# First casts off GpSimd, weights prepared later, scores of a head pair in two halves: fused attention and gated unit on one core

## Chip, cores and metric

One core of a Trainium2 chip. The metric is device time in microseconds (us) of one execution of the program, the median of several runs; one more execution was recorded by the profiler.

## What is computed

Attention over 8 batches, 8 heads, 576 positions and 64 channels, causal by blocks of 64 positions, and behind it a gated unit on the attention output laid out as 512 channels:

```python
scores = scale * np.matmul(q, k.transpose(0, 1, 3, 2))
scores = np.where(mask, scores, -1000000000.0)      # mask: block_i >= block_j
...
x = attn_out.transpose(0, 2, 1, 3).reshape(B, S, H * D)
for k in range(5):
    gate_pre += conv_w[k] * xp[:, k:k + S, :]       # xp: x with 4 rows of zeros ahead
out = (sigmoid(gate_pre) * (x @ w_val)) @ w_out
```

## The kernel before

The work is cut into 32 **steps**; step t handles one pair of heads of batch t // 4. Query and key arrive in **blocks** of four heads (`load_pair`, L393): a block feeds two steps, so steps 0 and 1 need block 0, steps 2 and 3 block 1, and so on. A load (`load_qk`, L90) is two DMAs on SyncE's queue and a cast from fp32 to fp16 (L99), on GpSimd but for the first. `load_v` (L102) is one DMA and eight copies of GpSimd, once per batch. `trans` (L121) turns a third of a block with TensorE (L129), and VectorE copies the result out of PSUM (L135).

A step's `scores` (L149) fill four PSUM buffers one after the other, of which two exist at a time; ScalarE takes the exponential of each (L163 twice at 1024 columns, L186 at 512, L163 at 320). When four steps are done, `den` (L206) sums the exponentials of the batch with 88 small matmuls (L237), and VectorE turns the sums into reciprocals, split in two bf16 parts (L244 to L249, ending in `comb`). `recips` (L253) spreads them with two matmuls per step (L259) that ScalarE copies out (L261), and `pv` (L265) makes the attention output, five steps behind the scores. `gate_val` (L314), nine steps behind, does the convolution as matmuls with diagonal weights (`diag`, L324), the gate (L327) and the value projection (L332); `project` (L340) the last product. All PSUM tiles but those of the scores come from one pool of four buffers (`psG`).

Before the loop stand the first two blocks, the first transposes, `consts`, `load_v(0)` and `weights` (L371): two weight loads on ScalarE's queue, a cast of each on GpSimd (L389), the convolution weights turned by four small fp32 matmuls (L375) and the 20 diagonal matrices (L380, GpSimd). In the loop (L427) come in turn the load of the next block, `load_v` of the next batch, the scores, the transposes of the block that follows, and `after` (L406).

The functions say what is done; a scheduler puts each engine's instructions into a fixed order, by its own estimates, when the program is built. At run time each engine works through its list in order, so an instruction that must wait holds up all behind it.

## Time and profile before

| | us |
|---|---|
| median of 3 runs | 287.13 |
| lowest, highest | 285.99, 287.56 |
| profiled execution, whole | 287.68 |
| profiled execution, span of the trace | 285.9 |
| TensorE busy in the span | 243.7 (85%) |
| ScalarE busy | 157.4 (55%) |
| VectorE busy | 143.6 (50%) |
| GpSimd busy | 102.7 (36%) |

PE is TensorE's matmul, PEld its weight load, DVE is VectorE, ACT ScalarE, POOL GpSimd, SP SyncE; a name with q behind it is the engine's queue. Times inside the trace count from the start of the span. A row of the timeline gives start, busy time, engine, line, operation, tiles, shape and count, and in brackets how long the engine had been idle and what ended that.

### The profile page before, as it was taken

The page shows a single profiled execution, that of the slowest core. Times are in us where ns is not written, and L with a number is a line of the kernel's source. Part 1 is how long each engine was busy: PE and PEld are TensorE (multiplying, and loading weights), DVE is VectorE, ACT ScalarE, POOL GpSimd, SP SyncE. Part 2 cuts the span into 40 slices and gives each one's busy share as a digit, 9 for nine tenths or more (in the row PEclk, how much of TensorE's full clock was granted, in tenths as well). Part 3 has the DMA queues.
Part 4 walks back from the last instruction along what each step waited for, and adds up shares of the span by engine and source line. Part 5 has one row for each costly group of instructions (what it writes and reads, how often), then busy time and mean ns, then how long its engine had stood idle before and what let it go on. Part 6 is the DMA issues. An engine that isn't in the chain of part 4 may idle for free.

```text
span 285.9 us, 7361 instructions
## 1 busy us (share of the span) xinstructions
PE 243.7 (85%) x3128; PEld 160.4 (56%) x3128; DVE 143.6 (50%) x257; ACT 157.4 (55%) x293; POOL 102.7 (36%) x129
## 2 busy tenths in 40 slices
PE   1672198796999998999899998999899999999994
PEld 1530164563666556666557556755667557667671
DVE  3730074579356835594438644683539324634230
ACT  1064048585476375728574575637584875444433
POOL 7379999917521911264113811182000000000000
PEclk9999999798699999999999999999999999999998
DMA  6999687999638587226933240001200210121214
GB/s 200 332 261 367 129 257 214 274 269 271 184 113 214 156 206 236 85 85 174 291 120 101 78 156 2 2 33 42 76 37 2 77 73 5 73 76 38 77 72 183
DMA packets 24842, 40.32 MB, mean 141 GB/s; under 512 B 1765, under 2 KB 10981, under 8 KB 24810
## 3 DMA queue, kind: packets, MB, share of 16 engines
q1 hardware_dynamic: 18560, 28.32, 35.2%
q10 hardware_dynamic: 6250, 11.55, 11.1%
q8 instruction: 24, 0.39, 0.6%
q14 instruction: 8, 0.07, 0.1%
HBM read 30.42 MB, written 9.44 MB: 139 GB/s over the span
## 4 chain that ended last, share of the span: by engine, by line
PE 58%; DVE 12%; ACT 11%; DMA 6%; issue 5%; POOL 3%; SPq 2%; ACTq 1%
PE cv L324 14%; PE vp L332 10%; PE ot L343 7%; PE x L304 7%; ACT pt L163 7%; PE ps L159 6%; DMA st<-in_k_dram 6%; PE dn L237 5%; DVE qkT L135 4%; PE tr L129 4%; ACT ob L347 3%; DVE hi L245 2%; SPq L95 2%; DVE ri L244 2%; POOL diag L380 1%
## 5 line engine op out<-in xcount | busy, mean ns | idle before, releaser
L163 ACT ACTIVATE pt<-ps 128x1024 f16<-128x1024 f32 (+1 forms) x96 | 77.7, 834 | 26.7 <-PE ps L159 23.8
L135 DVE COPY qkT<-tr 128x768 f16<-128x768 f16 (+1 forms) x64 | 50.3, 836 | 44.6 <-PE tr L129 44.4
L99 POOL CAST t<-st 128x1152 f16<-128x1152 f32 x31 | 35.1, 1145 | 69.3 <-PE tr L129 63.3
L336 DVE SCALAR_TENSOR_TENSOR gv<-th,vp 128x288 f16<-128x288 f32 x64 | 28.9, 452 | 35.0 <-PE vp L332 34.0
L129 PE MATMUL tr<-ident_59,t 128*128 128x128 f16 x288 | 26.6, 244 | 21.5 <-POOL t L99 15.1
L159 PE MATMUL ps<-qkT 64*128 64x64 f16 (+7 forms) x256 | 37.2, 312 | 7.6 <-ACT pt L163 4.5
L327 ACT ACTIVATE th<-cv 128x288 f32<-128x288 f32 x64 | 26.1, 415 | 31.5 <-PE cv L324 31.2
L347 ACT COPY ob<-ot 128x512 f32<-128x512 f32 x36 | 21.1, 585 | 36.5 <-PE ot L343 34.5
L324 PEld LDWEIGHTS <-diag 128*128 128x128 f16 x320 | 29.0, 98 | 15.9 <-issue 7.3
L343 PE MATMUL ot<-w_out_sb,gv 128*128 128x512 f16 x144 | 34.7, 380 | 1.7 <-DVE gv L336 1.7
L129 PEld LDWEIGHTS <-t 128*128 128x128 f16 x288 | 19.3, 109 | 27.9 <-POOL t L99 16.3
L304 PE MATMUL x<-pt,t 128*64 128x256 f16 (+3 forms) x384 | 30.7, 260 | 3.7 <-DVE qkT L135 3.0
L261 ACT COPY rb<-ps 128x288 f32<-128x288 f32 x64 | 23.6, 409 | 11.3 <-PE ps L259 10.9
L332 PEld LDWEIGHTS <-w_val_sb 128*128 128x128 f16 x256 | 25.0, 98 | 6.8
L186 ACT ACTIVATE pt<-ps 128x512 f16<-128x512 f32 x32 | 19.4, 605 | 14.3 <-PE ps L184 12.7
L304 PEld LDWEIGHTS <-t 128*64 128x64 f16 x384 | 18.8, 112 | 11.8 <-issue 6.6
L108 POOL CAST t<-st 128x2304 f16<-128x2304 f32 x8 | 16.9, 2106 | 20.5 <-PE x L304 18.3
L343 PEld LDWEIGHTS <-gv 128*128 128x128 f16 x144 | 13.7, 98 | 16.6 <-DVE gv L336 3.7
L159 PEld LDWEIGHTS <-qkT 64*128 64x128 f16 x256 | 11.7, 97 | 19.6 <-issue 13.4
L244 DVE RECIPROCAL ri<-dn 128x288 f32<-128x288 f32 x8 | 15.7, 1958 | 8.8 <-PE dn L237 8.5
L306 DVE TENSOR_TENSOR xb_69<-x,rb 128x320 f16<-128x320 f32 (+1 forms) x24 | 10.1, 444 | 17.0 <-ACT rb L261 15.3
L324 PE MATMUL cv<-xb_69,diag 128*128 128x288 f16 x120 | 18.4, 300 | 0.0
(93 smaller groups left out, 332.1 us busy)
## 6 DMA issues: line engine op xcount, KB each, us to landing
st<-in_q_dram SPq DMA_DIRECT2D x32, 288.0 KB, 3.9
st<-in_k_dram SPq DMA_DIRECT2D x32, 288.0 KB, 4.4
out_dram<-ob ACTq DMA_DIRECT2D x36, 256.0 KB, 2.0
st<-in_moe_w_val_dram ACTq DMA_DIRECT2D x1, 1024.0 KB, 9.9
st<-in_moe_w_out_dram ACTq DMA_DIRECT2D x1, 1024.0 KB, 7.4
st<-in_v_dram SPq DMA_DIRECT2D x8, 0.2 KB, 9.3
conv_nat<-in_moe_conv_w_dram ACTq DMA_DIRECT2D x1, 10.0 KB
```

Source lines behind the costliest of these rows:

```text
L99: eng.tensor_copy(out=t[:, :, :, :], in_=st[:, :, :, :].rearrange("p z c d -> p c z d"))
L129: nc.tensor.transpose(out=tr[:, s, :], in_=q16[hb, w][:, c, :, :], identity=ident16[:, :])
L135: nc.vector.tensor_copy(out=qkT[b][:, 2 * half:2 * half + 2, w, :].rearrange("p n (x c) -> p n x c", c=9)[:, :, :, c0:c0 + len(ss)], in_=t ...
L159: mm(out=ps[:, h, lo:lo + S - f], lhsT=kT[h][:, f - 64:f + 64], rhs=qT[h][:, f:S], start=True, stop=True, skip_group_check=True)
L163: nc.scalar.activation(out=pt[:, o:o + w], in_=src, func=AF.Exp, bias=0.0, scale=0.125)
L304: mm(start=(z == 0), stop=(z == len(x_) - 1), skip_group_check=True, **x_[z])
L324: mm(out=cv[:, :], lhsT=diag[:, g, j, :], rhs=xb[:, g, HF * hf + j:HF * hf + j + HF], start=(j == 0), stop=(j == 4), skip_group_check=True)
L327: nc.scalar.activation(out=th[:, HF * hf:HF * hf + HF], in_=cv[:, :], func=AF.Tanh, bias=0.0, scale=0.5)
L332: mm(out=vp[:, :], lhsT=w_val_sb[:, fc, 128 * g:128 * g + 128], rhs=xb[:, fc, 4 + HF * hf:4 + HF * hf + HF], start=(fc == 0), stop=(fc == ...
L336: nc.vector.scalar_tensor_tensor(out=gvs[u][:, g, c0:c0 + HF], in0=th[:, HF * hf:HF * hf + HF], scalar=1.0, in1=vp[:, :], op0=ALU.add, op1 ...
L343: mm(out=ot[:, :], lhsT=gvs[u][:, fc, 128 * j:128 * j + 128], rhs=w_out_sb[:, fc, :], start=(fc == 0), stop=(fc == 3), skip_group_check=True)
L347: nc.scalar.copy(out=ob[:, :], in_=ot[:, :])
```

## The change

The key cast of block 0 goes to ScalarE (the query cast was on VectorE already). `weights` is split: the convolution weights are prepared at step 3, with the 20 diagonal matrices on VectorE in place of GpSimd; the two large weights are loaded on SyncE's queue, the first at step 2 and the second at step 4. The second block's load and `load_v(0)` are asked for behind the first transposes. `scores` is called twice per step: two PSUM buffers first, then, behind the transposes, `recips`, `den` and `pv`, the other two.

```diff
-        eng = nc.vector if hb == 0 and w == 0 else nc.gpsimd
-        eng.tensor_copy(out=t[:, :, :, :], in_=st[:, :, :, :].rearrange("p z c d -> p c z d"))
+        cast = (nc.vector.tensor_copy, nc.scalar.copy)[w] if hb == 0 else nc.gpsimd.tensor_copy
+        cast(out=t[:, :, :, :], in_=st[:, :, :, :].rearrange("p z c d -> p c z d"))
...
-    def scores(t):
+    def scores(t, part):
...
+        if part == 0:
+            ps = psS.tile([128, 2, 512], fp32, tag="S")
+            full(ps, 0, 0, 0)
...
+            ex(1024, ps[:, :, :], 1024)
+            return
...
-                nc.gpsimd.tensor_scalar(out=diag[:, g, j, :], in0=ident16[:, :],
+                nc.vector.tensor_scalar(out=diag[:, g, j, :], in0=ident16[:, :],
...
+    def weights(w):
...
+        nc.sync.dma_start(out=st.rearrange("p (f n) -> p f n", f=4),
...
+    nc.scalar.dma_start(out=conv_nat[0:5, 0:512], in_=moe_conv_w[:, :])
     load_pair(0)
-    load_pair(1)
     for part in range(3):
         trans(0, part)
+    load_pair(1)
+    load_v(0)
     consts()
-    load_v(0)
-    weights()
...
+    for t in range(NT + 9):
         b, r = divmod(t, 4)
+        if t < NT:
+            scores(t, 0)
+        if t % 2 == 0:
+            load_pair(t // 2 + 2)
+        if t in (2, 4):
+            weights(t // 2 - 1)
+        if t == 3:
+            conv_weights()
+        if r == 1 and b + 1 < B:
+            load_v(b + 1)
+        if t < NT and t // 2 + 1 < 2 * B:
+            for part in ((0, 1), (2,))[t % 2]:
+                trans(t // 2 + 1, part)
+        if 0 <= t - 5 < NT:
+            recips(t - 5)
         if r == 0 and 1 <= b <= B:
             den(b - 1)
         if 0 <= t - 5 < NT:
-            recips(t - 5)
             pv(t - 5)
+        if t < NT:
+            scores(t, 1)
```

Three places show what this does to the fixed orders. The first is GpSimd's list before, from the casts of block 0's keys and block 1 (L99) to those of blocks 2 and 3.

```order
L99 CAST t<-st 128x1152 x3
L389 TENSOR_SCALAR w_val_sb<-st 128x2048
L380 TENSOR_SCALAR diag<-ident_59,convT 128x128 x3
L108 CAST t<-st 128x2304
L110 CAST d<-st 64x1024
L112 CAST d<-st 64x4x64 x4
L114 CAST vz_72<-st 64x4x320
L115 CAST vz_72<-st 64x4x64
L380 TENSOR_SCALAR diag<-ident_59,convT 128x128 x17
L389 TENSOR_SCALAR w_out_sb<-st 128x2048
L99 CAST t<-st 128x1152 x4
```

The same list now, from the last of the eight copies of batch 0's values on; ahead of it stand the two casts of block 1 and the other seven copies.

```order
L115 CAST vz_72<-st 64x4x64
L99 CAST t<-st 128x1152 x2
L108 CAST t<-st 128x2304
L110 CAST d<-st 64x1024
L112 CAST d<-st 64x4x64 x4
L114 CAST vz_73<-st 64x4x320
L115 CAST vz_73<-st 64x4x64
L99 CAST t<-st 128x1152 x2
L391 TENSOR_SCALAR w_val_sb<-st 128x2048
L99 CAST t<-st 128x1152 x2
L391 TENSOR_SCALAR w_out_sb<-st 128x2048
```

Block 2's casts moved ahead of all weights, but block 3's now stand behind the copies of batch 1's values, which they were ahead of.

The second place is TensorE's list where `den` of batch 0 begins; before, with the transposes of block 3 (tr_473) ahead of it and step 3's third score buffer (ps_403) amid it:

```order
L129 LDWEIGHTS t_343
L129 MATMUL tr_473<-ident16_59,t_343 128x128
L237 LDWEIGHTS oh_60
L237 MATMUL dn_482<-pt_242,oh_60 32x5x32
...
L237 MATMUL dn_482<-pt_242,oh_60 32x256
L159 LDWEIGHTS qkT_146
L159 MATMUL ps_403<-qkT_146 128x256
```

Now the same place follows the last score buffer of step 5 (ps_655) and the first transposes of block 3 (tr_449):

```order
L197 MATMUL ps_655<-qkT_328 64x64
L129 LDWEIGHTS t_318
L129 MATMUL tr_449<-ident16_59,t_318 128x128
...
L240 LDWEIGHTS oh_60
L240 MATMUL dn_466<-pt_200,oh_60 32x5x32
```

Steps 4 and 5 moved from amid and behind `den` of batch 0 to ahead of it. In the same way step 9's scores, which stood behind `den` of batch 1, stand ahead of it now, all but its last two small matmuls.

The third place is VectorE's list around the diagonal matrices (L382), between the copies of blocks 1 and 2 (ahead) and of block 3 (behind), as it is now:

```order
L135 COPY qkT<-tr 128x2x64x6 x2
L135 COPY qkT<-tr 128x2x64x3 x2
L379 COPY convT<-ps 128x20
L135 COPY qkT<-tr 128x2x64x6
L382 TENSOR_SCALAR diag<-ident_59,convT 128x128 x20
L135 COPY qkT<-tr 128x2x64x6
L135 COPY qkT<-tr 128x2x64x3 x2
L247 RECIPROCAL ri<-dn 128x288
L135 COPY qkT<-tr 128x2x64x6
```

The 20 multiplications came in ahead of block 3's copies and of the first reciprocal. On ScalarE the one table load, which stood first, now stands behind the landing of block 0's keys, in front of their cast.

## Rows read from the trace of the kernel before

**Rows 1.** The page: TensorE's busy tenths in 40 slices of the span.

```profile
PE   1672198796999998999899998999899999999994
```

**Rows 2.** The waits of the whole span: us in total, times, longest.

```profile
PE tr L129 <- POOL t L99: 15.1, 3, 11.7
```

**Rows 3.** Timeline 0 to 50 us, GpSimd and TensorE: start, us, engine, line, operation.

```profile
19.42 2.10 POOL L108 CAST t<-st 128x2304 f16<-128x2304 f32 x1 [1.60 <-DMA st<-in_v_dram]
...
25.81 5.92 POOL L380 TENSOR_SCALAR diag<-ident_59,convT 128x128 f16<-128x128 f16 x17
...
31.70 1.90 POOL L389 TENSOR_SCALAR w_out_sb<-st 128x2048 f16<-128x2048 f32 x1
33.54 4.41 POOL L99 CAST t<-st 128x1152 f16<-128x1152 f32 x4
...
34.74 1.38 PE L129 MATMUL tr<-ident_59,t 128*128 128x128 f16 x10 [11.67 <-POOL t L99]
```

**Rows 4.** Timeline 0 to 25 us: table load, first key cast, first scores, exponentials.

```profile
5.24 1.28 ACT L163 ACT_TABLE_LOAD   x1 [5.24 <-DMA st<-in_q_dram]
...
7.78 1.14 POOL L99 CAST t<-st 128x1152 f16<-128x1152 f32 x1 [1.90 <-DMA st<-in_k_dram]
...
10.05 1.87 PE L375 MATMUL ps<-ident,conv_nat 5*128 5x5 f32 x8
...
15.39 1.03 PE L159 MATMUL ps<-qkT 64*128 64x512 f16 x7
...
19.47 1.94 ACT L163 ACTIVATE pt<-ps 128x1024 f16<-128x1024 f32 x2 [0.19 <-PE ps L159]
...
22.63 1.94 ACT L163 ACTIVATE pt<-ps 128x1024 f16<-128x1024 f32 x2 [0.22 <-PE ps L159]
```

**Rows 5.** Windows: stretch; busy PE, PEld, DVE, ACT, POOL; PE clock, DMA share, GB/s.

```profile
10.00:20.00 10.00, 7.49 (x54) 5.00 (x53) 5.00 (x8) 3.50 (x5) 5.80 (x7) 1.00 1.07 288
```

**Rows 6.** The page's DMA issues: count, KB each, us to landing.

```profile
st<-in_moe_w_val_dram ACTq DMA_DIRECT2D x1, 1024.0 KB, 9.9
```

**Rows 7.** Timeline 43 to 62 us: step 4, sums, reciprocal, exponentials of steps 6 to 8.

```profile
43.39 1.03 PE L159 MATMUL ps<-qkT 64*128 64x512 f16 x7
...
44.35 0.85 PE L237 MATMUL dn<-pt,oh 128*32 128x192 f16 x21
...
46.92 1.96 DVE L244 RECIPROCAL ri<-dn 128x288 f32<-128x288 f32 x1 [4.95 <-PE dn L237]
...
50.19 1.94 ACT L163 ACTIVATE pt<-ps 128x1024 f16<-128x1024 f32 x2 [0.15 <-PE ps L159]
...
57.66 1.94 ACT L163 ACTIVATE pt<-ps 128x1024 f16<-128x1024 f32 x2 [0.88 <-PE ps L159]
...
60.95 1.94 ACT L163 ACTIVATE pt<-ps 128x1024 f16<-128x1024 f32 x2
```

**Rows 8.** Timeline 62 to 72 us: sums of batch 1 and what follows them.

```profile
63.32 1.38 PE L237 MATMUL dn<-pt,oh 128*32 128x128 f16 x76
...
64.75 1.96 DVE L244 RECIPROCAL ri<-dn 128x288 f32<-128x288 f32 x1 [0.64 <-PE dn L237]
...
70.49 0.92 PE L159 MATMUL ps<-qkT 64*128 64x512 f16 x5 [1.67 <-DVE qkT L135]
...
71.35 0.66 PE L259 MATMUL ps<-comb,sel 128*128 128x288 bf16 x2
```

**Rows 9.** Timeline: one VectorE cast beside a GpSimd copy, and the same cast alone.

```profile
66.10 2.11 POOL L108 CAST t<-st 128x2304 f16<-128x2304 f32 x1 [6.65 <-PE x L304]
...
66.97 1.39 DVE L245 CAST hi<-ri 128x288 bf16<-128x288 f32 x1
...
244.45 0.30 DVE L245 CAST hi<-ri 128x288 bf16<-128x288 f32 x1
```

**Rows 10.** TensorE's waits from 75 to 215 us.

```profile
PE ps L159 <- ACT pt L163: 2.3, 11, 0.2
...
PE ps L190 <- ACT pt L163: 0.8, 4, 0.2
```

More of the change, by code (lines that the diff above doesn't have):

```diff
@@ L147, in first_q @@
         return 2 * i + 1 + h
-    def scores(t):
+    def scores(t, part):
         b, n = divmod(t, 4)
-        pt = ptp.tile([128, 2880], fp16, tag="pt")
-        pts[t] = pt
+        if part == 0:
+            pts[t] = ptp.tile([128, 2880], fp16, tag="pt", name="pt")
+        pt = pts[t]
         hs = (slice(0, 64), slice(64, 128))
@@ L164, in ex @@
                                  scale=0.125)
-        ps = psS.tile([128, 2, 512], fp32, tag="S")
-        full(ps, 0, 0, 0)
-        full(ps, 1, 0, 0)
-        full(ps, 1, 3, 448)
-        ex(0, ps[:, :, :], 1024)
-        ps = psS.tile([128, 2, 512], fp32, tag="S")
-        full(ps, 0, 1, 0)
-        full(ps, 1, 1, 0)
-        full(ps, 0, 3, 384)
-        full(ps, 1, 2, 320)
-        ex(1024, ps[:, :, :], 1024)
+        if part == 0:
+            ps = psS.tile([128, 2, 512], fp32, tag="S")
+            full(ps, 0, 0, 0)
+            full(ps, 1, 0, 0)
+            full(ps, 1, 3, 448)
+            ex(0, ps[:, :, :], 1024)
+            ps = psS.tile([128, 2, 512], fp32, tag="S")
+            full(ps, 0, 1, 0)
+            full(ps, 1, 1, 0)
+            full(ps, 0, 3, 384)
+            full(ps, 1, 2, 320)
+            ex(1024, ps[:, :, :], 1024)
+            return
         ps = psS.tile([128, 2, 512], fp32, tag="S")
@@ L369, in consts, with conv_weights @@
                     in_=rs[:, 2 * h:2 * h + 2, r:r + 1].to_broadcast([128, 2, 64]))
-    def weights():
-        nc.scalar.dma_start(out=conv_nat[0:5, 0:512], in_=moe_conv_w[:, :])
+    def conv_weights():
         ps = psG.tile([128, 4, 16], fp32, tag="G")
@@ L379, in weights @@
             for j in range(5):
-                nc.gpsimd.tensor_scalar(out=diag[:, g, j, :], in0=ident16[:, :],
+                nc.vector.tensor_scalar(out=diag[:, g, j, :], in0=ident16[:, :],
                                         scalar1=convT[:, g, j:j + 1], scalar2=0.0,
                                         op0=ALU.mult, op1=ALU.add)
-        for w in range(2):
-            st = vstp.tile([128, 36, 64], fp32, tag="vst")
-            st = st[:, 0:32, :].rearrange("p t d -> p (t d)")
-            nc.scalar.dma_start(out=st.rearrange("p (f n) -> p f n", f=4),
-                                in_=(moe_w_val, moe_w_out)[w].rearrange("(f p) n -> p f n", p=128))
-            dst = (w_val_sb, w_out_sb)[w][:, :, :].rearrange("p f n -> p (f n)")
-            nc.gpsimd.tensor_scalar(out=dst, in0=st, scalar1=(1.0, 0.5)[w], scalar2=0.0,
-                                    op0=ALU.mult, op1=ALU.add)
+    def weights(w):
+        st = vstp.tile([128, 36, 64], fp32, tag="vst")
+        st = st[:, 0:32, :].rearrange("p t d -> p (t d)")
+        nc.sync.dma_start(out=st.rearrange("p (f n) -> p f n", f=4),
+                          in_=(moe_w_val, moe_w_out)[w].rearrange("(f p) n -> p f n", p=128))
+        dst = (w_val_sb, w_out_sb)[w][:, :, :].rearrange("p f n -> p (f n)")
+        nc.gpsimd.tensor_scalar(out=dst, in0=st, scalar1=(1.0, 0.5)[w], scalar2=0.0,
+                                op0=ALU.mult, op1=ALU.add)
     def load_pair(hb):
@@ L424, in after @@
                 project(*proj.pop(0))
-    proj = []
-    for t in range(NT + 9):
-        b, r = divmod(t, 4)
-        if t % 2 == 0:
-            load_pair(t // 2 + 2)
-        if r == 1 and b + 1 < B:
-            load_v(b + 1)
-        if t < NT:
-            scores(t)
-            if t // 2 + 1 < 2 * B:
-                for part in ((0, 1), (2,))[t % 2]:
-                    trans(t // 2 + 1, part)
-        after(t)
     while proj:
```

8 lines of the change are left out of this document (4 added, 4 removed).

## Prediction

> **What bounds the kernel now.** I read the page's slices first, then the waits, then the timeline of the first 75 us, last the waits of the long middle part. The slices [rows 1] show two programs. From slice 11 on (about 71 us) TensorE is busy nine tenths and more nearly to the end: there its own work is the bound. Ahead of that stand thin slices, the fourth and fifth almost empty. The waits name it: TensorE waited for a cast of GpSimd, L99, 11.7 us at the longest [rows 2]. The timeline tells why [rows 3]: the values of batch 0 landed at 19.42, GpSimd copied them until 25.81, made 17 diagonal matrices (5.92 us) and the fp16 copy of a weight (1.90 us), and only then, at 33.54, cast block 2. TensorE stood until 34.74 with step 2 half done. In the middle part TensorE hardly waits for ScalarE: 2.3 and 0.8 us in 140 us [rows 10].
>
> **The change, part by part.** The sum is made against the profiled execution, 287.68 us, which is 0.55 above the median of the runs.
>
> *First casts.* Block 0's keys were cast by an idle GpSimd from 7.78 to 8.92 [rows 4]. ScalarE must now first load its table, 1.28 us, which has come behind the landing; the cast itself I put at 1.1 us, from 0.97 for 1024 columns (half of 1.94) times 1152/1024. So the keys are ready at 10.2, 1.3 us later than before. That costs nothing: step 0 started only at 15.39, since the transposes of block 1 stood ahead of it. Now they stand behind for the most part, and nine transposes and a copy after 10.2 let step 0 start at about 12.4. From there ScalarE paces the steps at 3.16 us each (19.47 to 22.63). GpSimd loses the cast, where it was waiting anyway.
>
> *Block 2's supply.* The 1024 KB of the first weight no longer run beside the first loads. At the 288 GB/s that the queues moved then [rows 5, 6] they took 3.6 us, so batch 0's values land between 15.8 (all of it returned) and 19.4 (none). I take 15.8, since the queue was full. GpSimd's eight copies take 25.81 - 19.42 = 6.4 us, the two casts 4.41/2 = 2.2: block 2 is ready at 24.4 instead of 35.7. The 11.7 us wait goes, and next late is block 2 itself, for step 3 reaches its transposes at about 23.
>
> *Step 4.* Behind block 2's keys TensorE has the rest of step 3's second buffer (0.5), transposes (0.4), the four convolution matmuls, formerly under a wait and now on the path (1.87 [rows 4]), six more transposes (0.75) and VectorE's copy (1.0). Step 4 starts at about 29.1, against 43.39 [rows 7]: 14.3 us ahead.
>
> *The lead shrinks at the first sums.* Before, `den` of batch 0 was woven into steps 3 to 5. Now it stands behind step 5 and behind block 3's transposes, as the order shows. Steps 4 and 5 go at ScalarE's 3.16 us; the last matmuls of step 5 end at about 35.4. Then come 1.4 us of transposes and 88 sums. These took 0.85/21 = 40 ns each at 44.35 and 1.38/76 = 18 ns at 63.32 [rows 7, 8]: TensorE's two clock levels, 1.2 and 2.4 GHz. With the many gaps ahead I take the lower, 3.5 us (1.6 at the upper). The reciprocal starts at 40.3 instead of 46.92, 6.6 us ahead. Block 3 now stands behind batch 1's copies. Block 2 and those values are 1.18 MB each by their shapes, 8.2 us at 288 GB/s, so they are there at 24.0; 24.4 and 6.4 of copies and 2.2 of casts make 33.0, before TensorE asks at 35.4: not limiting.
>
> *And again at the second sums.* From the first reciprocal to `recips` of batch 1 took 71.35 - 46.92 = 24.4 us. There TensorE had step 9's scores to do while VectorE worked through the reciprocal (64.75 to 71.35, 6.6 us), and still idled 1.67 us [rows 8]. Now step 9 stands ahead of the sums and nothing but one attention output behind them. Counted from the reciprocal: 3.3 to step 6's exponentials, as before; 8.1 to step 7's (7.5 before, 50.19 to 57.66; the third buffer now follows twelve transposes, 0.6); 6.4 for steps 7 and 8 (3.3 before, 57.66 to 60.95, the pace of ScalarE); 1.9 for two exponentials of step 9; 1.1 for the transposes and the buffer ahead of the sums; 1.6 for the sums; 6.6 for the chain. That is 29.0, 4.6 us more than before. The lead that comes out is **2.0 us** (-1.6 if the values land at 19.4, 3.9 if the sums run at the upper level).
>
> *The middle.* From there both kernels have the same work left, and TensorE is the bound. Two score buffers, then other work, then two buffers, can remove at most the 2.3 + 0.8 us; at least nothing, since the scheduler had already woven attention between them. I take half, **1.5 us**. Moving `recips` ahead of `den` costs nothing: `pv` needs its results as early as before.
>
> *Weights on SyncE's queue.* They wait there for GpSimd to free a buffer, and block 4 and batch 2's values queue behind them. The first weight is issued when batch 0's copies end (22.2), the second when batch 1's end (30.8), batch 2's values after the first weight's cast (34.9). With both the second weight and the values still to move then (3.6 and 4.1 us at 288 GB/s) they land by 42.6; 6.4 of copies and 2.2 of casts make block 5 ready by 52. TensorE asks for it at step 9, around 60. Hidden, by 8 us.
>
> *Diagonals on VectorE.* 20 operations between 29.1 and the copies of block 3. They must be done by 38.0, for those copies take 2.3 us and the reciprocal is due at 40.3. The trace shows no such operation on VectorE; the smallest cast alone takes 0.30 us [rows 9], which makes 6 us: hidden by the steps 4 and 5. If the cover goes, every us is on the path.
>
> The sum is 287.68 - 2.0 - 1.5 = 284.2; less 0.55 for the median, **283.7 us**.
>
> **Rivals.**
>
> *A: VectorE waits for GpSimd (slower or none).* `hi` took 0.30 us with GpSimd idle, and 1.39 beside a GpSimd copy, ending 0.15 after it: 66.97 + 1.39 = 68.36, against 66.10 + 2.11 = 68.21 [rows 9]. So a VectorE operation between SBUF tiles can wait for the copy in flight. From 29.1 GpSimd has eight copies and casts on end (two of batch 1, blocks 3 and 4, both weights), to 39.0. If one diagonal gets through after each, twelve are left at 39.0, done at 42.6, block 3's copies at 44.9: the reciprocal 4.6 us later, 283.7 + 4.6 = 288.3. It decides from the point where the diagonals end after 38.0. For it: the `hi` rows. Against: several diagonals may pass at each gap, for they follow each other without a dependence. The Trainium skill's page "GPSIMD Engine Reference" (Key points) says that GpSimd shares its SBUF interfaces with VectorE and contends with VectorE instructions that run in a two-port mode or have two SBUF inputs; by it the diagonals would contend as `hi` did, and the time would be this rival's.
>
> *B: the lead stays (faster).* If the gap after the second sums is filled or the sums run at the upper clock level, the 6.6 us remain: 287.13 - 6.6 - 1.5 = 279.0. For it: step 9's exponentials are done early, so that ScalarE can run ahead. Against: step 10 needs the copy that stands behind the reciprocal on VectorE, and TensorE works in order.
>
> *C: nothing arrives.* If the values land at 19.4 as before, the lead is -1.6, and with the middle's 1.5 the time is 287.2.
>
> **How the numbers follow.** What a measurement can tell from no change is 0.5%, 1.4 us. Chances: forecast 0.48, own range 281.5 to 286; A 0.27, 286 to 289.5; B 0.17, 277.5 to 281.5; C 0.08. Faster (under 285.7) holds most of the forecast, 0.41, all of B, and little of the rest: 0.60. Slower (over 288.6) holds a third of A and of C: 0.12. The rest, 0.28, is no difference. Leaving a tenth out on each side the range is 278.5 to 288.7.
>
> **What would show it.** Right: no wait of TensorE on L99 over 3 us; the first reciprocal near 40.3; the second 22.4 us behind it; a TensorE gap of 4 us behind the second sums; from there a distance to the end about 1.5 us shorter than before. A: diagonals that end with GpSimd's copies, and the last after 38. B: less than 25 us from the first reciprocal to `recips` of batch 1. Wrong: a wait in the middle that was not there, or block 5 late.

## The result: nearly three times the gain forecast, and in another place

The changed kernel takes 277.55 us (median of 4 runs, 276.93 to 279.85), the kernel before 287.02 beside it (4 runs): a ratio of 0.9689, interval 0.9626 to 0.9751. The forecast was 283.7, its range 278.5 to 288.7. The gain is 9.5 us, where 3.4 were forecast, and the time lies outside the range. (Medians below are over all runs of a kernel; ratios leave disturbed runs out.) The profiled execution took 277.92 us, its span is 276.1.

The page of the changed kernel: busy time by engine, TensorE's busy tenths and granted clock in 40 slices of 6.9 us.

```profile
PE 240.4 (87%) x3128; PEld 162.4 (59%) x3128; DVE 149.9 (54%) x277; ACT 158.4 (57%) x294; POOL 94.4 (34%) x108
...
PE   0588774977699998999899999999999999999994
...
PEclk9999998986599999999999999999999999999998
```

The slices next to [rows 1] show a start that fills earlier: the empty fourth and fifth are gone. But slices 7 to 11 are thinner for the most part, and the full stretch begins no sooner. The timeline of the changed kernel tells both halves of the story, the start in detail, then two places of the middle (columns as in the rows ahead of the prediction).

```profile
16.43 2.11 POOL L108 CAST t<-st 128x2304 f16<-128x2304 f32 x1 [4.03 <-DMA st<-in_v_dram]
...
22.80 2.23 POOL L99 CAST t<-st 128x1152 f16<-128x1152 f32 x2
...
30.05 1.03 PE L160 MATMUL ps<-qkT 64*128 64x512 f16 x7 [0.45 <-ACT pt L189]
...
29.57 10.01 DVE L382 TENSOR_SCALAR diag<-ident_59,convT 128x128 f16<-128x128 f16 x20
39.50 2.14 DVE L135 COPY qkT<-tr 128x768 f16<-128x768 f16 x3
41.51 1.93 DVE L247 RECIPROCAL ri<-dn 128x288 f32<-128x288 f32 x1
...
44.30 0.61 PE L160 MATMUL ps<-qkT 64*128 64x512 f16 x7 [3.75 <-DVE qkT L135]
...
46.34 2.10 POOL L108 CAST t<-st 128x2304 f16<-128x2304 f32 x1 [3.97 <-DMA st<-in_v_dram]
...
62.72 2.86 PE L240 MATMUL dn<-pt,oh 128*32 128x160 f16 x88
...
65.65 1.96 DVE L247 RECIPROCAL ri<-dn 128x288 f32<-128x288 f32 x1 [1.71 <-PE dn L240]
...
71.17 0.93 PE L160 MATMUL ps<-qkT 64*128 64x512 f16 x5 [3.79 <-DVE qkT L135]
72.03 0.66 PE L262 MATMUL ps<-comb,sel 128*128 128x288 bf16 x2
...
120.26 1.96 DVE L247 RECIPROCAL ri<-dn 128x288 f32<-128x288 f32 x1 [0.46 <-PE dn L240]
...
133.31 0.61 PE L160 MATMUL ps<-qkT 64*128 64x512 f16 x7
133.85 0.84 PE L129 MATMUL tr<-ident_59,t 128*128 128x128 f16 x12
...
178.15 1.96 DVE L247 RECIPROCAL ri<-dn 128x288 f32<-128x288 f32 x1 [0.46 <-PE dn L240]
```

Step 4 starts at 30.05 against 43.39 [rows 7], the first reciprocal at 41.51 against 46.92: the lead is there. Then it is lost. The reciprocals of batch 1 are spread (L262) at 72.03 against 71.35 [rows 8], so the start as a whole is 0.7 us *later*. From there to the end the changed kernel needs 276.1 - 72.03 = 204.1 us, the kernel before 285.9 - 71.35 = 214.5. **All of the gain, 10.4 us, is in the middle**, where the forecast allowed 3.1 at most. None of it lies behind the last reciprocal (232.47 now, 242.23 before): from there both kernels take 43.7 us to the end.

The middle repeats itself every two batches, so one such stretch can stand for it. The same stretch of the kernel before, from the timeline, with a few score matmuls in it:

```profile
122.87 1.96 DVE L244 RECIPROCAL ri<-dn 128x288 f32<-128x288 f32 x1 [0.64 <-PE dn L237]
...
124.17 0.79 PE L324 MATMUL cv<-xb_70,diag 128*128 128x288 f16 x5
124.89 0.39 PE L159 MATMUL ps<-qkT 64*128 64x512 f16 x1
125.21 0.79 PE L324 MATMUL cv<-xb_70,diag 128*128 128x288 f16 x5
125.83 1.14 PE L332 MATMUL vp<-xb_70,w_val_sb 128*128 128x288 f16 x8
...
132.56 0.81 PE L159 MATMUL ps<-qkT 64*128 64x512 f16 x4
133.34 0.28 PE L324 MATMUL cv<-xb_71,diag 128*128 128x288 f16 x1
...
137.37 0.39 PE L159 MATMUL ps<-qkT 64*128 64x320 f16 x4
137.69 0.29 PE L180 MATMUL ps<-qkT 64*64 64x256 f16 x1
...
185.24 1.96 DVE L244 RECIPROCAL ri<-dn 128x288 f32<-128x288 f32 x1 [0.65 <-PE dn L237]
```

Two batches, from the fourth reciprocal to the sixth, take 185.24 - 122.87 = 62.37 us before and 178.15 - 120.26 = 57.89 after. The windows of these two stretches, first before, then after (stretch; length, then busy PE, PEld, DVE, ACT, POOL; clock, DMA share, GB/s):

```profile
122.87:185.24 62.37, 58.22 (x781) 37.94 (x780) 36.16 (x58) 38.53 (x73) 22.33 (x24) 1.00 0.37 115
```

```profile
120.26:178.15 57.89, 55.49 (x783) 37.48 (x783) 35.07 (x59) 38.37 (x73) 22.33 (x24) 1.00 0.41 125
```

The work is the same and so is the clock, 1.00 of full speed, yet TensorE's **busy** time fell by 2.7 us, more than half of the 4.5. So what was removed had been counted as work. The rows show how that can be. A matmul's row lasts until its modelled end, 0.2 us and more behind the point where the next one could start: the four score matmuls at 132.56 show 0.81 us and no idle time, and next comes 133.34. They took 0.78 from start to start; the other three of this first half came at 137.37, in a group of four that took 0.32. After the change the seven stand together and take 133.85 - 133.31 = 0.54.

I therefore read each matmul from its start to the next one's start, over the two stretches. Of this time I call *matmul* its columns at 0.417 ns each and 2.5 ns besides (128 columns take 0.056 us, 512 take 0.216, and 288 take 0.122: 125.21 to 125.83 is five), plus 0.097 us where the next matmul uses the array in another shape; where the time goes beyond both by more than 25 ns, the excess is a *wait*. The shapes are the whole array, 64 rows (scores), 64 columns (attention output) and 32 columns (sums). A change of shape shows at 124.17: five matmuls of 288 columns take 0.72 us with a score behind them, and 0.62 at 125.21 with none. Over the stretch of the kernel before the medians are 95 to 112 ns by kind of change. The Trainium skill, page "TensorEngine Tiling (Array Packing)", section "Key Properties", says that changing the tiling mode, and not just the tile, drains the engine; the trace agrees in that each such change takes time, 0.1 us.

By this account two batches of the kernel before are 54.9 us of matmuls with 62 changes of shape and 7.4 us of waits; of the changed kernel 53.4 with 58 changes and 4.5 of waits. So **2.9 us of the 4.5 are waits and 1.6 are matmul time**; the largest part of the 1.6 is the scores, 8.1 us before and 7.3 after. The waits view of the stretch before (us in total, times, longest) names 3.6 of the 7.4 us:

```profile
PE x L304 <- DVE qkT L135: 1.5, 2, 0.7
PE ot L343 <- DVE gv L336: 0.9, 2, 0.4
PE ps L159 <- ACT pt L163: 0.8, 4, 0.2
PE ps L190 <- ACT pt L163: 0.4, 2, 0.2
```

### The profile page after: what moved, and what is told of

It reads as the page before. It is cut to its first block, busy times and chain, and to the rows that moved or that the text cites. A ratio compares the mean times of both kernels' runs of the same rounds, so it can differ in the third digit from the quotient of the medians.

```text
span 276.1 us, 7368 instructions
## 1 busy us (share of the span) xinstructions
PE 240.4 (87%) x3128; PEld 162.4 (59%) x3128; DVE 149.9 (54%) x277; ACT 158.4 (57%) x294; POOL 94.4 (34%) x108
## 4 chain that ended last, share of the span: by engine, by line
PE 60%; DVE 15%; ACT 8%; issue 6%; DMA 4%; POOL 3%; SPq 2%; ACTq 1%; POOLq 0%
PE cv L327 14%; PE vp L335 10%; PE ot L346 7%; PE x L307 7%; PE ps L160 5%; PE tr L129 5%; DVE qkT L135 5%; PE dn L240 5%; ACT pt L164 4%; DMA st<-in_v_dram 4%; DVE diag L382 4%; ACT ob L350 3%; DVE ri L247 2%; PE ps L262 2%; SPq L95 2%
## 5 line engine op out<-in xcount | busy, mean ns | idle before, releaser
L99 POOL CAST t<-st 128x1152 f16<-128x1152 f32 x30 | 34.0, 1144 | 61.9 <-PE tr L129 57.2
L339 DVE SCALAR_TENSOR_TENSOR gv<-th,vp 128x288 f16<-128x288 f32 x64 | 28.9, 452 | 37.2 <-PE vp L335 35.6
L160 PE MATMUL ps<-qkT 64*128 64x512 f16 (+7 forms) x256 | 35.1, 315 | 15.3 <-DVE qkT L135 8.3
L330 ACT ACTIVATE th<-cv 128x288 f32<-128x288 f32 x64 | 26.9, 421 | 21.6 <-PE cv L327 20.3
L327 PEld LDWEIGHTS <-diag 128*128 128x128 f16 x320 | 28.8, 98 | 10.6 <-issue 1.8
L307 PE MATMUL x<-pt,t 128*64 128x256 f16 (+3 forms) x384 | 29.7, 261 | 2.8 <-DVE qkT L135 2.2
L129 PEld LDWEIGHTS <-t 128*128 128x128 f16 x288 | 19.9, 111 | 16.6 <-DVE t L99 6.5
L160 PEld LDWEIGHTS <-qkT 64*128 64x128 f16 x256 | 12.4, 97 | 27.9 <-issue 14.5
L307 PEld LDWEIGHTS <-t 128*64 128x64 f16 x384 | 18.1, 113 | 10.4 <-issue 5.8
L189 ACT ACTIVATE pt<-ps 128x512 f16<-128x512 f32 x32 | 20.2, 632 | 3.0 <-PE ps L197 2.7
```

The costliest lines, as they stand in the source:

```text
L99: cast(out=t[:, :, :, :], in_=st[:, :, :, :].rearrange("p z c d -> p c z d"))
L129: nc.tensor.transpose(out=tr[:, s, :], in_=q16[hb, w][:, c, :, :], identity=ident16[:, :])
L160: mm(out=ps[:, h, lo:lo + S - f], lhsT=kT[h][:, f - 64:f + 64], rhs=qT[h][:, f:S], start=True, stop=True, skip_group_check=True)
L307: mm(start=(z == 0), stop=(z == len(x_) - 1), skip_group_check=True, **x_[z])
L327: mm(out=cv[:, :], lhsT=diag[:, g, j, :], rhs=xb[:, g, HF * hf + j:HF * hf + j + HF], start=(j == 0), stop=(j == 4), skip_group_check=True)
L330: nc.scalar.activation(out=th[:, HF * hf:HF * hf + HF], in_=cv[:, :], func=AF.Tanh, bias=0.0, scale=0.5)
```

## Experiments

### Which part of the change makes it: e1_halves, e2_start, e3_whole

*e1_halves* is the kernel before with the two-part `scores` of the changed kernel and its order of calls (here without their conditions):

```diff
+            scores(t, 0)
             load_pair(t // 2 + 2)
...
-            scores(t)
...
                     trans(t // 2 + 1, part)
-            den(b - 1)
             recips(t - 5)
+            den(b - 1)
             pv(t - 5)
+            scores(t, 1)
```

> The kernel before with one part of the change only: the scores in two halves and the new order of the loop (first half, transposes, reciprocals, sums, attention output, second half). First casts, weights and diagonals stay as they were. Theory M (the gain lies in the middle: TensorE's short waits for the exponentials vanish in every step, 10.4 us from the first reciprocals of batch 1 to the end): 276 to 278.5 us, all of the gain, as the changed start brought its first reciprocals of batch 1 0.7 us later and not earlier. Theory S (the earlier supply of the first steps is needed for it, since weights and diagonals no longer stand between the loads): 282 us or more.

*e2_start* is the changed kernel with the loop of the kernel before (again without conditions):

```diff
-            scores(t, 0)
             load_pair(t // 2 + 2)
...
+            scores(t, 0)
+            scores(t, 1)
...
-            recips(t - 5)
             den(b - 1)
+            recips(t - 5)
             pv(t - 5)
-            scores(t, 1)
```

> The changed kernel with its start (first casts on VectorE and ScalarE, weights in the loop and on SyncE's queue, diagonals on VectorE), but with the scores of a step undivided and the loop in the old order. Theory M: the start is worth nothing, 286 to 289 us (287.0 plus the 0.7 us by which the changed kernel's first reciprocals of batch 1 come later). Theory S: at most 282 us, half of the gain or more.

*e3_whole* moves only the second half, to the first:

```diff
             scores(t, 0)
+            scores(t, 1)
...
-            scores(t, 1)
```

> The changed kernel with both halves of a step's scores called one behind the other where the first half stands; the rest of the order (transposes, then reciprocals, sums, attention output) and the start stay as changed. Theory M in its narrow form (what counts is that work lies between the two halves): 285 to 289 us, no gain left. Theory O (the reciprocals of a step ahead of the sums and their copies on ScalarE make it): at most 281 us.

Measured, with 287.73 for the kernel before: e1_halves 276.82 us, ratio 0.9604 (0.9577 to 0.9630). e2_start 288.83, 1.0040 (1.0000 to 1.0079). e3_whole 285.08, 0.9933 (0.9904 to 0.9963). Theory M holds for the place: the halves and the order carry the whole gain, the new start carries none, and neither needs the other. e3_whole lies at the lower end of what the narrow form allowed and outside theory O's range. Still, against e2_start the new order with undivided scores brings 3.75 us (285.08 against 288.83), so the order has a share of its own. It has `recips` ahead of `den` and the scores ahead of the loads; these two were not tried apart. In e2_start two batches take 62.31 us, as before the change. The stretch of two batches in e3_whole:

```profile
120.95:181.44 60.49, 56.82 (x783) 37.49 (x783) 35.11 (x58) 38.38 (x73) 22.36 (x24) 1.00 0.38 117
```

60.49 lies between 62.37 and 57.89: by the account the order takes matmuls from 54.9 to 53.8 us (59 changes, and the scores in larger pieces) and waits from 7.4 to 6.7; the halves then take off 2.2 us of waits and 0.4 of matmuls.

### Which waits: f1_before_short, f2_halves_short

The kernel before (f1) and e1_halves (f2), each with ScalarE's exponentials cut to half of their columns, all four kinds as this one; each ran once:

```diff
-            ex(0, ps[:, :, :], 1024)
+            ex(0, ps[:, :, 0:256], 512)
```

> The kernel before, with each exponential over half of its columns only (1024 to 512, 512 to 256, 320 to 160; the other half of each probability tile stays at 1.0 from a fill on VectorE at the start, which delays the start). Read from the third reciprocal after the start-up to the last (122.87 to 242.23 in the kernel before: 119.4 us; 119.19 to 231.40 in the kernel before with halves: 112.2 us). Theory W (in the middle TensorE waits for the exponentials, in pieces that the waits view does not show): with exponentials of half the length this stretch falls to 112 to 114 us, nearly as far as the halves bring it. Theory P (the halves change how fast TensorE itself runs the same matmuls, or other queues): it stays at 117 to 119.5 us.

> The kernel before with the scores in halves and the new loop order, and with each exponential over half of its columns only, as in the run beside it. Theory W: the waits are gone already, so the stretch between the same two reciprocals, 112.2 us with full exponentials, stays at 110 to 112.5. Theory P: no forecast of its own, but a fall by 3 us or more would mean that ScalarE still sets the pace with the halves.

The shorter instructions also made the scheduler choose another order, so that these two are no clean cut. Fourth and last reciprocal of f1_before_short, from the timeline:

```profile
131.63 1.96 DVE L244 RECIPROCAL ri<-dn 128x288 f32<-128x288 f32 x1
...
247.08 1.96 DVE L244 RECIPROCAL ri<-dn 128x288 f32<-128x288 f32 x1 [1.02 <-PE dn L237]
```

The same of f2_halves_short:

```profile
124.37 1.96 DVE L247 RECIPROCAL ri<-dn 128x288 f32<-128x288 f32 x1 [0.48 <-PE dn L240]
...
231.79 1.96 DVE L247 RECIPROCAL ri<-dn 128x288 f32<-128x288 f32 x1 [1.26 <-PE dn L240]
```

The stretch is 115.4 us in the first (119.4 with full exponentials) and 107.4 in the second (112.2). f1 lies between the ranges of its two theories. f2's stretch fell by 4.8 us, below theory W's range; a fall of 3 or more was to mean that ScalarE still sets the pace with the halves. Shorter exponentials gain 4 to 5 us in *both*, so the halves do not take all the waits that ScalarE's exponentials cause, and what they gain, 7.2 us, is still there (8.0) when the exponentials are short. By the account the waits of two batches fall from 7.4 to 5.4 and from 4.5 to 2.7. My theory W was too simple. How much of the 4 to 5 us comes from the other order is not shown.

### Where the second half stands: g1_behind_trans

```diff
             trans(t // 2 + 1, part)
+        if t < NT:
+            scores(t, 1)
...
-        if t < NT:
-            scores(t, 1)
```

> The changed kernel with the second half of the scores called right behind the transposes, ahead of reciprocals, sums and attention output. Theory W: the 6 or 12 transposes between the halves, 0.4 to 0.8 us, cover less than half of the first two exponentials (1.94 us), so most of the halves' gain over the undivided scores is lost: 281 to 285 us. Rival C (it is enough that the two halves are apart at all): 277 to 279 us.

284.86 us, ratio 0.9898 (0.9858 to 0.9938): in the range that W gave, for a reason it did not give. The stretch of two batches takes 59.97 us:

```profile
124.50:184.47 59.97, 57.87 (x783) 37.80 (x782) 34.82 (x58) 38.49 (x73) 22.33 (x24) 1.00 0.38 119
```

TensorE is busy for 57.87, 2.4 us more than in the changed kernel with the same matmuls. The waits are 4.6, as good as the changed kernel's 4.5; but the scheduler now cuts the work into smaller pieces, with 72 changes of shape, and the matmuls take 55.4 instead of 53.4. By the account this place loses by smaller pieces and their shape changes, not by waits.

### Does the order inside a half matter: p1_unpaired

```diff
-            full(ps, 0, 0, 0)
             full(ps, 1, 0, 0)
             full(ps, 1, 3, 448)
+            full(ps, 0, 0, 0)
...
             full(ps, 0, 1, 0)
-            full(ps, 1, 1, 0)
             full(ps, 0, 3, 384)
+            full(ps, 1, 1, 0)
             full(ps, 1, 2, 320)
```

> The changed kernel with the score matmuls of the first half called head by head (second head, first head; first head, second head) instead of in turns, nothing else moved. In the trace of the changed kernel a score matmul of one head starts 3 to 7 ns after one of the other head, and the seven of a first half take 0.54 us together, though 2048 columns at 0.42 ns each, the pace of the 288-column matmuls (0.122 us), would take 0.85. Theory Q (the two heads' matmuls, 64 rows each, run side by side on TensorE, so what stands next to what decides how long scores take): the seven take 0.78 to 0.87 us, two batches take 59.7 to 60.6 us instead of 57.9, and the time is 284 to 288 us. Rival W (only waits for the exponentials count): no change, 276.5 to 279 us.

278.72 us, ratio 0.9723 (0.9654 to 0.9792): no change, and theory Q's price was wrong. The two rows of its timeline:

```profile
134.29 0.61 PE L160 MATMUL ps<-qkT 64*128 64x448 f16 x7
134.83 0.84 PE L129 MATMUL tr<-ident,t 128*128 128x128 f16 x12
```

The seven take 0.54 us again. They do run side by side (0.54 for 2048 columns), but TensorE brings the two heads together by itself within a piece: the 512-column matmul of one head, called third, starts 6 ns behind the first, ahead of the second. What is left as a reason for shorter scores is how many pieces they are cut into.

### Fewer shape changes, and what they cost: j1_order

On the best kernel so far (h2_start, below), TensorE held to the order of the loop from step 10 on:

```diff
+    def pin(i):
+        if step[0] >= 10:
+            tc.keep_in_program_order(i)
...
-            mm(out=ps[:, :, :], lhsT=sel[:, n, e, :, :], rhs=combs[b][:, :], start=True,
-               stop=True, skip_group_check=True)
+            pin(nc.tensor.matmul(out=ps[:, :, :], lhsT=sel[:, n, e, :, :], rhs=combs[b][:, :], start=True,
+               stop=True, skip_group_check=True))
```

> The kernel of the run h2_start (272.26 us) with TensorE's instructions kept in the order of the loop from step 10 on, so that the scheduler no longer puts pieces of other work between the score and attention-output matmuls. By the traces so far, TensorE loses about 0.1 us whenever the shape of the array part in use changes (full, 64 rows for scores, 64 columns for the attention output, 32 for the sums): medians of 95 to 112 ns beyond the columns at 0.42 ns each, in every kernel. Two batches of h2_start hold 58 such changes and take 57.84 us; in loop order they hold 42. Theory Z (the changes count and the waits stay): two batches take 56.0 to 56.6 us, and the time is 267 to 269. Rival W (the pieces stood where TensorE would have waited for an exponential or a copy, so the waits take it all back and more): two batches take 58 to 61 us, and the time is 272.5 to 281.

276.42 us against h2_start's 272.26; ratio to the kernel before 0.9604 (0.9573 to 0.9636). The stretch of two batches in h2_start:

```profile
115.12:172.96 57.84, 55.50 (x783) 37.48 (x783) 35.06 (x59) 38.35 (x73) 22.34 (x24) 1.00 0.41 124
```

The same stretch in j1_order:

```profile
120.56:179.91 59.35, 53.73 (x783) 36.31 (x783) 35.03 (x59) 38.20 (x73) 22.36 (x24) 1.00 0.41 121
```

And its largest wait there (us in total, times, longest):

```profile
PE x L313 <- DVE qkT L141: 4.1, 8, 0.7
```

Both theories are half right, and this run separates the two terms. The 16 changes fewer are worth 2.9 us of matmuls (53.4 to 50.5; busy time falls by 1.8), nearly 0.2 each: 16 changes at 0.097 are 1.6 us, and the scores, no longer cut up, fall from 7.3 to 6.0. The waits rise from 4.5 to 8.9, most of it ahead of the attention output, for buffers of `psG` that VectorE's copies of the transposes free. So the scheduler's small pieces had stood where TensorE would have waited.

### Taking those waits away: i1_proj, k1_spread, k2_spread_free, k3_apart

*i1_proj*, on the changed kernel: projections ahead of the gate.

```diff
+        for _ in range(2):
+            if proj:
+                project(*proj.pop(0))
         m = t - 9
         if 0 <= m < NT:
             gate_val(*divmod(m, 4))
...
-        for _ in range(2):
-            if proj:
-                project(*proj.pop(0))
```

> The changed kernel with the projections of a step called ahead of the gate of that step instead of behind it, so that a projection never reads what VectorE has just gated. In the changed kernel the first projection behind a gate waits 0.2 to 0.4 us for VectorE (0.73 us per two batches between start and start). Theory W (such short waits count in full): 1 to 3 us faster than the changed kernel, 274.5 to 276.5. Rival N (the wait moves to the next matmul that needs VectorE, or the last projections make the tail longer): 276.5 to 279.

Ratio 0.9702 (0.9668 to 0.9736), no change from 0.9689. Two batches take 58.30 us instead of 57.89: rival N. The wait moved to the reciprocals; the largest wait of the stretch (us in total, times, longest):

```profile
PE ps L262 <- DVE comb L252: 2.5, 2, 1.2
```

*k1_spread* puts the calls of j1_order into another order from step 10 on (conditions left out); *k2_spread_free* is the same without holding TensorE to it.

```diff
+            recips(t - 5)
             scores(t, 0)
-            transposes(t)
-            recips(t - 5)
             den(b - 1)
             pv(t - 5)
+            transposes(t)
+            gate(t)
             scores(t, 1)
-            gate(t)
             projects()
```

*k3_apart* changes k1_spread once more; `inverse` is VectorE's part of `den`, its reciprocal held to this place.

```diff
             pv(t - 5)
+            inverse(b - 1)
             transposes(t)
-            gate(t)
+            projects()
             scores(t, 1)
-            projects()
+            gate(t)
```

> The kernel j1_order (TensorE in loop order from step 10 on) with another loop order from step 10: reciprocals of a step, first half of the scores, sums, attention output, transposes, gate, second half of the scores, projections. Between start and start the matmuls of two batches take 50.5 us in j1_order when each slot over its columns and shape change is cut out, and 8.9 us of waits stand beside them, most ahead of the attention output, for buffers that VectorE's copies of the transposes free. Account A (waits plus changes of shape are all there is): the 42 changes stay, so the matmuls take 50 to 51 us again; the transposes now lie behind the attention output and both halves have more than 2 us of other work behind them, so waits of 1 to 4 us are left; two batches take 51.5 to 54.5 us, and the time is 255 to 266 us. Rival B (the four shared accumulator buffers make a new wait wherever the transposes stand): waits of 6 us or more, two batches at 57 us or more, 270 us or more.

> The same loop order without holding TensorE to it: the scheduler may put pieces of other work in between (204 changes of shape in the program instead of 170; h2_start has 210). Account A: the matmuls take 53 to 54 us per two batches as in h2_start (53.4), with waits of 1 to 4 us, so 54.5 to 57.5 and 262 to 271 us, slower than k1_spread by 2 us or more. Rival B: as in h2_start or slower, 272 us or more.

> The kernel k1_spread with the projections of a step between its transposes and the second half of its scores, the gate last, and VectorE's reciprocal of the sums behind the two products of the attention output instead of ahead of them. In k1_spread the matmuls of two batches took 50.5 us as forecast, but 9.2 us of waits stood beside them, nearly all in the one step in four that has the sums: VectorE's chain of 3.6 us from the reciprocal on delayed products, copies and gate there (1.0 us in the transposes, 1.7 us in the projections, 0.5 in the gate). Account A: matmuls 50 to 51 us, waits of 1.5 to 5 us, two batches 51.5 to 56 us, the time 255 to 268 us. Rival B: the chain delays the copies of the transposes or the next reciprocals instead, waits of 6 us or more, two batches at 57 us or more, 270 us or more.

| | us | ratio (interval) | two batches | changes | matmuls | waits |
|---|---|---|---|---|---|---|
| before | 287.02 | 1 | 62.4 | 62 | 54.9 | 7.4 |
| changed kernel | 277.55 | 0.9689 (0.9626, 0.9751) | 57.9 | 58 | 53.4 | 4.5 |
| j1_order | 276.42 | 0.9604 (0.9573, 0.9636) | 59.4 | 42 | 50.5 | 8.9 |
| k1_spread | 277.46 | 0.9686 (0.9647, 0.9724) | 59.7 | 42 | 50.5 | 9.2 |
| k2_spread_free | 274.77 | 0.9604 (0.9547, 0.9661) | 59.0 | 55 | 52.8 | 6.2 |
| k3_apart | 283.13 | 0.9794 (0.9711, 0.9878) | 61.6 | 42 | 51.1 | 10.6 |

Matmul time goes with the pieces and is separate from the waits: at 42 changes it was 50.5, 50.5 and 51.1 us, whatever the order of the steps, as account A said. The stretch of k3_apart runs from the fifth reciprocal to the seventh, and 6.9 us of it at 1.2 GHz; with the columns counted at that level there, its matmuls are 53.6 us and its waits 8.0. Account A's second half fell three times, and rival B's terms were met each time: I could not place the waits. In k1_spread they gather in the one step in four that has the sums (`ot` behind the gate 3.1 us, transposes 1.6), in k3_apart TensorE waits for the spread reciprocals, 2.3 us twice. VectorE's chain behind the sums always meets something. None beats h2_start.

### The start: e4_diag_gp, h1_start, h2_start

*e4_diag_gp* puts the diagonals back on GpSimd:

```diff
-                nc.vector.tensor_scalar(out=diag[:, g, j, :], in0=ident16[:, :],
+                nc.gpsimd.tensor_scalar(out=diag[:, g, j, :], in0=ident16[:, :],
```

> The changed kernel with the 20 diagonals back on GpSimd, all else as changed. Theory D (the 10.01 us of diagonals on VectorE hold the first reciprocal and block 3's copies, and what that costs lasts to the end): the first reciprocal starts near 40.2 instead of 41.51, TensorE's 3.75 us wait ahead of step 6 shrinks below 2, and the time falls to 274 to 276. Theory G (GpSimd sets the pace of the first two batches: its 18 diagonals of 0.37 us, 6.7 us, now stand ahead of the value copies of batch 1 and the casts of blocks 5 and 6): the first reciprocals of batch 1 come 1 to 5 us later than 72.03 and the time is 278 to 283.

283.88 us, ratio 0.9854 (0.9831 to 0.9878), worse than theory G's upper end. From its timeline:

```profile
28.64 6.32 POOL L382 TENSOR_SCALAR diag<-ident,convT 128x128 f16<-128x128 f16 x18 [3.19 <-DVE convT L379]
...
47.26 1.96 DVE L247 RECIPROCAL ri<-dn 128x288 f32<-128x288 f32 x1 [1.24 <-PE dn L240]
```

And from its waits between 30 and 92 us (us in total, times, longest):

```profile
PE tr L129 <- POOL t L99: 5.7, 1, 5.7
```

GpSimd waited 3.19 us for the multiplier, then spent 6.32 on diagonals with the values of batch 1 and block 3 behind them, and TensorE waited 5.7 us for block 3, which it does not in the changed kernel. So diagonals on VectorE, though they took 10.01 us, were worth some 5 us against the same place on GpSimd (0.9854 against 0.9689).

*h1_start* leaves the diagonals on GpSimd, makes them wait for the first reciprocals (`late` is 1.0), and moves them and the second weight back; *h2_start* is the same with the diagonals at step 6 and the second weight at step 11.

```diff
-        nc.vector.tensor_copy(out=convT[:, :, :], in_=ps[:, :, 0:5])
+        nc.vector.tensor_scalar(out=late[:, :], in0=combs[0][:, 0:1], scalar1=0.0, scalar2=1.0,
+                                op0=ALU.mult, op1=ALU.add)
+        nc.vector.tensor_scalar(out=convT[:, :, :], in0=ps[:, :, 0:5], scalar1=late[:, 0:1],
+                                scalar2=0.0, op0=ALU.mult, op1=ALU.add)
...
-        if t in (2, 4):
-            weights(t // 2 - 1)
-        if t == 3:
-            conv_weights()
+        if t == 2:
+            weights(0)
...
+        if t == 9:
+            weights(1)
...
+        if t == 7:
+            conv_weights()
```

> The changed kernel with another start: the 20 diagonals on GpSimd but only in step 7, behind the casts of block 5 (their multiplier waits for the first reciprocals), and w_out loaded in step 9 instead of step 4, so that the values of batch 2 get their buffer as soon as batch 1's are copied. Theory G (GpSimd's queue sets the pace of the first two batches): the first reciprocal starts near 40.2, the values of batch 2 are copied from about 39 instead of 46.34, blocks 5 and 6 come 4 us or more earlier, the first reciprocals of batch 1 come near 68 instead of 72.03, and the time is 273 to 275 us. Rival T (TensorE's work and its granted clock in the first 72 us set that pace, not the supply): 276.5 to 278.5 us.

h1_start: 276.07 us, ratio 0.9624 (0.9584 to 0.9664). The first reciprocal came at 39.55 and the second at 60.76, 4.9 us ahead of the changed kernel's 65.65; but the third only at 90.26. The time lies between the two theories' ranges, and its interval overlaps the changed kernel's. GpSimd and VectorE in its timeline:

```profile
55.26 6.97 POOL L386 TENSOR_SCALAR diag<-ident,convT 128x128 f16<-128x128 f16 x20 [3.52 <-DVE convT L382]
62.17 2.23 POOL L100 CAST t<-st 128x1152 f16<-128x1152 f32 x2
...
62.97 4.62 DVE L249 CAST hi<-ri 128x288 bf16<-128x288 f32 x1
```

TensorE's largest wait between 40 and 92 us (us in total, times, longest):

```profile
PE ps L161 <- DVE qkT L136: 7.0, 2, 4.9
```

GpSimd stood 3.52 us for the multiplier, with block 6 behind the diagonals. In the expectation of h2_start, below, I took the wait of 4.9 us for one on block 6, and that is wrong: TensorE turns block 6 only from 76.29, without a wait. It waited, until 69.46, for VectorE's copy of block 5, which stands behind the cast `hi`. That cast takes 0.30 us alone [rows 9]; here it took 4.62, to 67.59, while GpSimd cast block 6 and copied values with no more than 0.1 us between.

> The changed kernel with the start of the run before (diagonals on GpSimd, behind the first reciprocals), with the diagonals one step earlier and the load of w_out in step 11, behind the loads of blocks 6 and 7 (in that run its issue held SyncE's queue 4.46 us ahead of block 6, and the diagonals waited 3.52 us for their multiplier ahead of block 6's casts). Theory G: block 6's casts end by 60 instead of 64.4, TensorE's wait of 4.9 us for them falls below 2, the third reciprocal starts near 87 instead of 90.26, and the time is 272 to 274.5. Rival T (the loads themselves, at 260 to 300 GB/s up to 60 us, hold batch 2): third reciprocal at 89.5 to 91, 275 to 277.5 us.

h2_start: **272.26 us, ratio 0.9482 (0.9462 to 0.9502), faster than both kernels.** GpSimd and VectorE in its timeline:

```profile
52.80 6.97 POOL L386 TENSOR_SCALAR diag<-ident,convT 128x128 f16<-128x128 f16 x20 [1.70 <-DVE convT L382]
59.71 2.23 POOL L100 CAST t<-st 128x1152 f16<-128x1152 f32 x2
...
86.59 1.96 DVE L248 RECIPROCAL ri<-dn 128x288 f32<-128x288 f32 x1 [0.46 <-PE dn L241]
```

Block 6 is cast 2.5 us earlier than in h1_start (61.9 in place of 64.4; 60 was expected), and the third reciprocal starts at 86.59, where 87 was expected and the changed kernel has 91.75. Its middle is the changed kernel's (57.84 us per two batches). So theory G's numbers came, and the changed kernel's start had some 5 us left in it; but the reason is not that blocks come too late. In all three kernels TensorE found blocks 5 and 6 cast, and block 6 is ready later here than in the changed kernel (61.9 against 57.1). Against h1_start, `hi` takes 0.84 us here in place of 4.62, and the wait of 4.9 us is 1.5.

Against the changed kernel, 2.1 of the 5.2 us are there at the first reciprocal (39.40 against 41.51), without diagonals on VectorE, and 4.3 at the second (61.34 against 65.65): its 88 sums took 1.61 us in place of 2.86. The granted clock from 60 to 90 us is 0.94 in the mean here and 0.78 in the changed kernel. How much of the gain is the clock was not tried apart.

## Why the prediction was wrong, step by step

**The middle** is the step that failed: "Two score buffers, then other work, then two buffers, can remove at most the 2.3 + 0.8 us." I took the two rows of the waits view that name ScalarE [rows 10] as the upper bound of what the halves can win. Over two batches the whole view names 3.6 of 7.4 us, since a wait that ends before the modelled end of the matmul ahead of it never shows as idle; and it says nothing of the 0.1 us per change of shape or of scores cut into pieces, which are busy time in every view. Term by term: 1.5 us taken, at most 3.1 allowed, 10.4 measured. The claim "there its own work is the bound" rested on nine busy tenths, and busy tenths do not tell a full engine from one with many small holes. The Trainium skill, page "Perfetto Trace Analysis", section "Identifying the Most-Contended Engine", warns that matmul busy time is no good measure of how near a kernel is to its limit. This case agrees: 58.22 us busy became 55.49 for the same matmuls. The page's reason, that pipelined instructions look smaller in the trace, is not what is seen here: a row looks longer than the matmul's slot, 0.81 us against 0.78 for the four scores at 132.56.

**First casts, block 2, step 4** were right. The values were copied from 16.43 (15.8 forecast), block 2 was ready at 22.80 + 2.23 = 25.0 (24.4), step 4 started at 30.05 (29.1; the terms listed for it add up to 28.9). The 11.7 us wait is gone, as forecast.

**The first reciprocal** came at 41.51 (40.3): rival A in part. The diagonals took 10.01 us for 20, where I reckoned 6 from a cast, and ended at 39.58, behind the 38.0 from which I said it decides. Taken one by one, they are of two kinds, with two in between. Twelve took 0.24 us each, less than the cast; the last five, with GpSimd idle, took 0.89 together. Six took 1.14 to 1.89 us, and each of these ended 0.04 to 0.06 us behind an instruction of GpSimd, as this one (GpSimd ahead, VectorE behind):

```profile
34.50 2.00 POOL L391 TENSOR_SCALAR w_val_sb<-st 128x2048 f16<-128x2048 f32 x1 [0.46 <-DMA st<-in_moe_w_val_dram]
34.66 1.89 DVE L382 TENSOR_SCALAR diag<-ident_59,convT 128x128 f16<-128x128 f16 x1
```

That is A's mechanism, and as A foretold the diagonals lasted as long as GpSimd's casts (36.45 + 2.27 = 38.7) and a little over; it cost 1.2 us against the forecast instead of 4.6, because several passed at the gaps. The page "GPSIMD Engine Reference" of the Trainium skill (Key points) names contention between the two engines for VectorE instructions in a two-port mode or with two SBUF inputs; the trace agrees that they contend, and does not show which of the two conditions holds here.

**The lead shrinks** was right in mechanism and a little short in size: from the first reciprocal to the second batch's spread reciprocals 72.03 - 41.51 = 30.5 us, against 29.0 forecast and 24.4 before; the gap behind the second sums is 3.79 us (4 forecast), the 88 sums took 2.86 us where I had put 1.6, at a granted clock of 0.67 in the mean between 60 and 70 us. The lead came out at -0.7 instead of 2.0, and e2_start measures the same by itself: no gain.

**Weights on SyncE's queue: "Hidden, by 8 us"** held, with less to spare. The values of batch 2 were copied from 46.34 (42.6 forecast), behind the second weight, and block 5 was cast by 54.9 (52); TensorE turned it from 60.14 (60), without a wait. That is 5.2 us to spare. With diagonals and second weight moved back, the third reciprocal still comes 5.2 us earlier (h2_start); which of the two moves brings how much was not tried apart.

**The order of `recips` and `den`, "costs nothing"**, missed a gain, or part of one: e3_whole beats e2_start by 3.75 us, with the scores ahead of the loads as well.

Rival B's time, 279.0, was the nearest, for a reason that did not occur: the lead did not stay.

## What to carry to other kernels

Where TensorE looks nine tenths full, read it from start to start before calling it the bound: sum columns at the granted clock, count the changes of array shape, and see what is left. Undivided small matmuls of one shape are worth keeping together, but only as long as the buffers behind them are free; in this kernel pieces put into gaps and gaps left open cost about the same. And look at whom preparation work meets, not just at which engine is free: on GpSimd it held up the cast that TensorE needed next (e4_diag_gp), and copies of GpSimd that run on end held up VectorE on the way to the next reciprocals (h1_start).

## What was not expected of the hardware

- A change of the array's shape (whole, 64 rows, 64 columns, 32 columns) costs TensorE about 0.1 us, medians of 95 to 112 ns by kind in the stretch of the kernel before, with nothing else to wait for.
- Score matmuls of the two heads (64 rows each) run side by side, 2048 columns in 0.54 us, and in p1_unpaired the third in order started ahead of the second.
- A small VectorE operation (128x128, fp16) took 0.24 us, and 1.14 to 1.89 where an instruction of GpSimd was under way; the same operation on GpSimd takes 0.35 (6.32 us for 18 in e4_diag_gp, 6.97 for 20 in h2_start). Behind GpSimd instructions that follow each other without a pause, one VectorE cast of 0.30 us took 4.62 (h1_start).
- In k3_apart, where TensorE stood 2.3 us in the middle of its work every four steps, the granted clock of these stretches fell to 0.94 and 0.95 in the mean; it is 1.00 in all the others of the table.
